# Left output products moved into the values pass and to the segment's end, and left products that lead only with resident units

## Chip, cores, metric

One core of one Trainium2 chip. The metric is the device time of one execution in us. The kernel before: 2348.51 us median of 3 runs (2346.82 to 2349.23). Every run lists the mean granted TensorE clock of the core. The views name the engines PE (TensorE), ACT (ScalarE), DVE (VectorE), POOL (GpSimd) and SP (SyncE, which issues the weight stream).

## The reference, cut to what matters

```python
for s in range(n_seg):                       # 64 segments of 32 tokens, one after the other
    xs = x[:, s * 32:(s + 1) * 32, :]
    h = concatenate([mem, xs])               # 8 memory rows + 32 token rows
    q, k, v = h @ Wq, h @ Wk, h @ Wv         # 1024 -> 32 heads x 128
    scores = where(mask, q k^T * scale, -1e9)
    o = softmax(scores) @ v
    o = o @ Wo                               # 4096 -> 1024
    mem = o[:, :8]                           # feeds the next segment
    outs.append(o[:, 8:])
# + x + gelu(xn @ w1 + b1) @ w2 + b2, xn = layernorm(x)
```

The layer norm and the dense part run first, in about 16% of the time. Then come the 64 segments. `mem` makes them a chain.

## The kernel before: what the argument touches

The weights are 64 units of 512 KB: eight units in each of K, Q, V for the first half of the heads, the same for the second half, then 16 output units. 43 stay resident in SBUF. 21 are streamed again in every segment, through six buffers.

```python
IS_STREAMED = {...}   # K 0,3,6; Q 1,4,7; V 2,5 of each half; output units 0,3,6,9,12

def unit_done(unit):
    if IS_STREAMED[unit]:
        start_stream()          # the buffer is free: the unit six places on is fetched
        ...
        # one or two small output writes are issued on POOL
```

Per segment, 24 token rows and the memory go through as "main" products (32 columns of weights loaded, hT). The last eight token rows of four segments in a row are joined into one "left" product (hL): left products are made in one segment of four. A segment has a kind 0 to 3 by its place in the group. Left K is made in kind 0, left Q in kind 2, left V in kind 3 (first half) and 0 (second half), left output in kind 3.

```python
def half_pass(w, u, left, at, lead=0):       # K is called with lead=3
    ...                                      # product() is left out
    for n in range(-lead, KT):
        if left and n + lead < KT:
            product(n + lead, hL, psL)       # leads by three units, streamed or not
        if n >= 0:
            product(n, hT, ps)
            unit_done((w, n, u))
            for fn in at.get(n, ()):
                fn()                         # attention steps between the products
    return ps, psL
...
lag = 3 if left_o else 0                     # output pass, kind 3
for n in range(16 + lag):
    if n < 16:
        o_product(n, [st["oT", 0], st.get(("oT", 1))], psX)
    if n == 15 and not final:
        nc.scalar.copy(out=o_sb[:, :], in_=psX[:, 0:256])   # making the tiles o_sb, res, resL is left out
    if left_o and n >= lag:
        o_product(n - lag, oL, psXL)         # left product, three units behind
    if n >= lag:
        unit_done(ORDER[48 + n - lag])
    for fn in at.get(n, ()):
        fn()
    if n == 7:
        nc.gpsimd.dma_start(out=res[:, :], in_=hr_d[s + 1, :, 256:512])
        if left_o:
            nc.gpsimd.dma_start(out=resL[:, :], in_=hrL_d[g + 1, :, 256:512])
if not final:
    put_mem(o_sb, nxt["hT"], ...)            # two transposes, DVE copy into hT: the new memory
nc.vector.tensor_tensor(out=res[:, :], in0=psX[:, 0:256], in1=res[:, :], op=ALU.add)
...                                          # with left_o, the addition for resL follows
```

The softmax here doesn't subtract the row's maximum and nothing guards it: scores larger than these inputs give would overflow.

Of the kernel before, what the change touches and what calls it, by code (L numbers as in the profile page):

```python
# [10 lines left out]
BF16 = mybir.dt.bfloat16  # L11
F32 = mybir.dt.float32
ACT = mybir.ActivationFunctionType
ALU = mybir.AluOpType
PSUM = bass.MemoryType.PSUM

P = 128
# [9 lines left out]
KT = DM // P  # L27
# [21 lines left out]
def pass_order():  # L49
# [14 lines left out]
ORDER = pass_order()  # L64
IS_STREAMED = {
    unit: (n * STREAMED + NUNIT - 1) // NUNIT != ((n + 1) * STREAMED + NUNIT - 1) // NUNIT
    for n, unit in enumerate(ORDER)
}
# [5 lines left out]
def kernel(  # L74
# [16 lines left out]
    nc = tc.nc  # L91
# [42 lines left out]
    for m, n, base in ((mask_order[0:NX, 0:NX], NX, 0), (mask_order[0:SEG, NX:SEG], NL, NX)):  # L134
        nc.gpsimd.affine_select(
            out=m, in_=m, pattern=[[1, n]], compare_op=ALU.is_ge, fill=MASKED, base=base, channel_multiplier=-1,
# [3 lines left out]
        out=m, in_=m, pattern=[[-8, GRP]], compare_op=ALU.is_ge, fill=MASKED, base=0, channel_multiplier=1,  # L140
    )
    nc.gpsimd.affine_select(
        out=m, in_=m, pattern=[[8, GRP]], compare_op=ALU.is_ge, fill=MASKED, base=7, channel_multiplier=-1,
# [58 lines left out]
    sp = ctx.enter_context(tc.tile_pool(name="sp", bufs=1))  # L202

    def put_mem(o_sb, hT, psM):

        for c in range(2):
            nc.tensor.transpose(psM[:, c, :], o_sb[:, c * P:(c + 1) * P], ident[:, :])
        nc.vector.tensor_copy(
            out=hT[:, :, NX:SEG].rearrange("p (j c) t -> p j c t", c=2),
            in_=psM[:, 0:2, :].rearrange("p c (j t) -> p j c t", j=4)[:, :, :, NX:SEG],  # L210
        )
# [3 lines left out]
    with tc.tile_pool(name="ma", bufs=2) as ma, tc.tile_pool(name="mps", bufs=6, space=PSUM) as mps:  # L215
# [11 lines left out]
        o_sb = sp.tile([P, 512], BF16, name="d")  # L227
# [18 lines left out]
        for i in range(14):  # L246
            t = slab(f"w2_{i}")[:, :].rearrange("p (c d) -> p c d", d=DM)
# [93 lines left out]
        for tg in range(4):  # L341
# [13 lines left out]
            for fb in range(FC):  # L355
                ps = mps.tile([P, 512], F32, name="ps")
                for kt in range(KT):
                    nc.tensor.matmul(  # L358
                        ps[:, :].rearrange("p (s t) -> p s t", t=SEG),
                        lhsT=w1_sb[fb // 14 * 8 + kt][:, (fb % 14) * P:(fb % 14 + 1) * P],  # L360
                        rhs=xnT[kt // 4][:, :, kt % 4, :],
                        start=(kt == 0),
                        stop=(kt == KT - 1),
# [3 lines left out]
                    out=xb[:, :], in_=ps[:, :], func=ACT.Identity, bias=b1col[:, fb:fb + 1], scale=1.0  # L367
                )
                u = ma.tile([P, 512], BF16, name="g_u")
                nc.vector.tensor_tensor(out=u[:, :], in0=xb[:, :], in1=xb[:, :], op=ALU.mult)  # L370
                nc.vector.tensor_scalar(
                    out=u[:, :], in0=u[:, :], scalar1=0.044715, scalar2=1.0, op0=ALU.mult, op1=ALU.add
# [7 lines left out]
            if tg == 0:  # L380
                for nb in range(2):
                    cs = slice(nb * 512, nb * 512 + 512)
                    ps = mps.tile([P, 512], F32, name="ps")
# [3 lines left out]
            if not last:  # L387
# [9 lines left out]
                for t in range(4):  # L397
# [3 lines left out]
                    for nb in range(2):  # L401
                        cs = slice(nb * 512, (nb + 1) * 512)
                        ps = mps.tile([P, 512], F32, name="ps")
# [56 lines left out]
    with tc.tile_pool(name="late", bufs=1) as late, \  # L460
# [7 lines left out]
        def unit_tile(unit):  # L468
            if IS_STREAMED[unit]:
                return stream_tiles.popleft()[:, :]  # L470
            return res_tiles[unit]
# [8 lines left out]
        def unit_done(unit):  # L480

            if IS_STREAMED[unit]:
                start_stream()
                if late_units:
                    fetch_late(late_units.popleft())
                for _ in range(2 if len(small) > 8 else 1):
                    if small:
                        small.popleft()()
# [6 lines left out]
        def by_head(t):  # L495
            return t.rearrange("p c (j t) -> p (c j) t", j=4)

        hT, hL = nxt["hT"], nxt["hL"]
        qL = qlp.tile([P, 8, P], BF16, name="qL")
        kL, VL, oL = [None] * 2, [None] * 2, [None] * 2  # L500
        for s in range(NSEG):
# [17 lines left out]
            def half_pass(w, u, left, at, lead=0):  # L519


                ps = accp.tile([P, 512], F32, name="acc")
                psL = accp.tile([P, 512], F32, name="acc") if left else None
                tiles = {}

                def product(i, lhs, acc):
                    if i not in tiles:
                        tiles[i] = unit_tile((w, i, u))
                    for j in range(4):
                        nc.tensor.matmul(  # L530
                            acc[32 * j:32 * j + 32, :],
                            lhsT=lhs[:, i, :],
                            rhs=tiles[i][:, 512 * j:512 * j + 512],
                            start=(i == 0),
                            stop=(i == KT - 1),
                            tile_position=(0, 32 * j),
                        )

                for n in range(-lead, KT):
                    if left and n + lead < KT:  # L540
                        product(n + lead, hL, psL)
                    if n >= 0:
                        product(n, hT, ps)
                        unit_done((w, n, u))
                        for fn in at.get(n, ()):
                            fn()
                return ps, psL

            def rows_out(ps, tag):
# [30 lines left out]
            def q_left(u):  # L580

                if i4 == 3 and more:
                    q = qS[:, u, :, :]
                else:
                    q = by_head(qL[:, 4 * u:4 * u + 4, :])[:, :, NL * i4:NL * i4 + NL]
                nc.vector.tensor_copy(out=st["qT"][:, :, 32:40], in_=q)
# [51 lines left out]
            def values(u, r):  # L638
# [22 lines left out]
                cp(out=st["oT", u][:, 2 * r:2 * r + 2, :, :], in_=oV[:, :, :, 0:32])  # L661
                cp(out=oL[u][:, 2 * r:2 * r + 2, :, NL * i4:NL * i4 + NL], in_=oV[:, :, :, 32:40])


            psK, psKL = half_pass("K", 0, left_k, {}, lead=3)
            nat = rows_out(psK, "d")
# [34 lines left out]
            if first:  # L701
                at[3].append(lambda: st.update(natL=left_out(psQ1L, "VL1", late)))
                at[5] = [lambda: turn_qL(st["natL"], 1), lambda: q_left(1)]
            else:
                at[3].append(lambda: q_left(1))
            psV1, psV1L = half_pass("V", 1, left_v[1], at)
            st["V"] = left_out(psV1, "a")
            if left_v[1]:
# [8 lines left out]
                at[8] = [lambda: st.update(natL=left_out(psQ1L, "d"))]  # L717
                at[11] = [lambda: turn_qL(st["natL"], 1)]
            psX = accp.tile([P, 512], F32, name="acc")
            psXL = accp.tile([P, 512], F32, name="acc") if left_o else None  # L720
            tiles = {}

            def o_product(n, lhs, acc):
                w, i, u = ORDER[48 + n]
                if n not in tiles:
                    tiles[n] = unit_tile((w, i, u))
                for k in range(2):
                    for jq in range(4):
                        nc.tensor.matmul(  # L729
                            acc[32 * jq:32 * jq + 32, 0:256],  # L730
                            lhsT=lhs[i // 4][:, i % 4, 2 * u + k, :],
                            rhs=tiles[n][:, 1024 * k + 256 * jq:1024 * k + 256 * jq + 256],
                            start=(n == 0 and k == 0),
                            stop=(n == 15 and k == 1),
                            tile_position=(0, 32 * jq),
                        )

            lag = 3 if left_o else 0
            res = resL = None
            for n in range(16 + lag):  # L740
                if n < 16:
                    o_product(n, [st["oT", 0], st.get(("oT", 1))], psX)
                if n == 15 and not final:
                    o_sb = sp.tile([P, 256], BF16, name="o_sb", tag="d")
                    nc.scalar.copy(out=o_sb[:, :], in_=psX[:, 0:256])
                if left_o and n >= lag:
                    o_product(n - lag, oL, psXL)
                if n >= lag:
                    unit_done(ORDER[48 + n - lag])
                for fn in at.get(n, ()):  # L750
                    fn()
                if n == 7:
                    res = sp.tile([P, 256], BF16, name="res", tag="e")
                    nc.gpsimd.dma_start(out=res[:, :], in_=hr_d[s + 1, :, 256:512])
                    if left_o:
                        resL = late.tile([P, 256], BF16, name="resL", tag="VL1")
                        nc.gpsimd.dma_start(out=resL[:, :], in_=hrL_d[g + 1, :, 256:512])
            if not final:
                put_mem(o_sb, nxt["hT"], trp.tile([P, 4, P], BF16, name="tr"))
            nc.vector.tensor_tensor(out=res[:, :], in0=psX[:, 0:256], in1=res[:, :], op=ALU.add)  # L760

# [2 lines left out]
                small.append(lambda o=o, r=res[32 * jq:32 * jq + NX, :]: nc.gpsimd.dma_start(out=o, in_=r))  # L764
            if left_o:
                rows_o = out_flat[g * GRP * SEG:(g + 1) * GRP * SEG, :].rearrange("(i t) d -> i t d", t=SEG)
                nc.vector.tensor_tensor(out=resL[:, :], in0=psXL[:, 0:256], in1=resL[:, :], op=ALU.add)

                for jq in range(4):
                    for i in range(GRP):  # L770
                        o = rows_o[i, NX:SEG, 256 * jq:256 * jq + 256]
                        r = resL[32 * jq + NL * i:32 * jq + NL * i + NL, :]
                        small.append(lambda o=o, r=r: nc.gpsimd.dma_start(out=o, in_=r))  # L773
# [37 lines left out]
```

## Time and profile before

| | before |
|---|---|
| time, median us | 2348.51 |
| TensorE busy, us | 2042.0 |
| moved by DMA, MB | 792.03 |
| group of four segments, mean us | 117.7 |
| kind 0, 1, 2, 3, mean us | 29.2, 28.1, 28.6, 31.8 |

The views are in the prediction. To read them: the stream of weights runs at about 407 GB/s when it is full (404 to 408 in the rows shown there). In one stretch of every group TensorE is nearly always busy and the stream starves (158 to 348 GB/s in the rows shown). That stretch goes from the output pass of kind 3 to V of the next kind 0.

### The profile page before, as it was taken

How to read it: one execution, taken by the hardware profiler on the slowest of the kernel's cores; microseconds unless marked ns; L12 is line 12 of the kernel's file. 1: busy time of each engine (PE TensorE's matmuls, PEld its weight loads, DVE VectorE, ACT ScalarE, POOL GpSimd, SP SyncE). 2: the span in 40 equal slices, each digit the busy share in tenths (PEclk: the TensorE clock that was granted, in tenths of full speed). 3: DMA queues.
4: the chain of work that ended last, by engine and by line, in shares of the span. 5: the costliest groups of instructions: out<-in, count | busy, mean ns of one | idle time of the engine just before them, and what ended most of it. 6: DMA issues, size and time to landing. Idle time of an engine off the chain costs nothing.

```text
span 2349.5 us, 84568 instructions
## 1 busy us (share of the span) xinstructions
PE 2042.0 (87%) x37759; PEld 1052.3 (45%) x37779; DVE 698.3 (30%) x1922; ACT 516.9 (22%) x1221; POOL 372.7 (16%) x745
## 2 busy tenths in 40 slices
PE   7999999788888888888888888888888888888885
PEld 3444444344444444444444444444444444444443
DVE  6574752122222222222222222222222222222221
ACT  5261432121111111111111211111111111111121
POOL 0000000023121212121212121212121212121212
PEclk9999999999999999999999999999999999999998
DMA  9521126899999999999999999999999999999996
GB/s 325 186 68 48 39 69 248 320 402 367 403 368 402 381 391 366 401 372 375 378 405 375 400 369 398 372 378 372 406 369 394 372 400 376 401 377 405 371 398 237
DMA packets 266408, 792.03 MB, mean 337 GB/s; under 512 B 55995, under 2 KB 71131, under 8 KB 266044
## 3 DMA queue, kind: packets, MB, share of 16 engines
q1 hardware_dynamic: 243004, 769.66, 85.2%
q0 software_dynamic: 22464, 15.92, 2.3%
q8 instruction: 295, 4.83, 0.8%
q10 hardware_dynamic: 576, 1.05, 0.1%
q14 instruction: 69, 0.57, 0.1%
HBM read 772.83 MB, written 29.88 MB: 342 GB/s over the span
## 4 chain that ended last, share of the span: by engine, by line
PE 49%; DMA 42%; issue 4%; DVE 3%; ACT 1%; POOL 1%; POOLq 0%; ACTq 0%; DVEq 0%; SPq 0%
DMA u<-Wc_Q 21%; PE acc L530 17%; DMA u<-Wc_O 11%; PE acc L729 9%; PE ps L358 8%; PE ps L405 6%; DMA u<-Wc_V 4%; DMA u<-Wc_K 3%; PE av L646 2%; DMA res<-hr_d 2%; PE tr L493 2%; PE ps L438 2%; PE av L652 1%; DVE natL L556 1%; PE pT L438 1%
## 5 line engine op out<-in xcount | busy, mean ns | idle before, releaser
L530 PE MATMUL acc<-u,hr 128*32 128x512 bf16 x12288 | 961.3, 388 | 111.0 <-DMA u<-Wc_Q 50.3
L530 PEld LDWEIGHTS <-hr 128*32 128x32 bf16 x12288 | 316.2, 96 | 434.5 <-issue 206.8
L530 PE MATMUL acc<-u,hrL 128*32 128x512 bf16 x3072 | 298.2, 384 | 22.2 <-DMA u<-Wc_V 10.3
L551 ACT CAST nat<-acc 128x512 bf16<-128x512 f32 x256 | 149.8, 585 | 558.9 <-PE acc L530 522.9
L729 PEld LDWEIGHTS <-oT 128*32 128x32 bf16 x8192 | 209.7, 97 | 93.1 <-issue 70.4
L729 PE MATMUL acc<-W_O,oT 128*32 128x256 bf16 x4096 | 184.2, 279 | 28.1 <-issue 27.9
L556 DVE CAST natL<-acc 128x512 bf16<-128x512 f32 x224 | 152.3, 686 | 187.1 <-PE acc L530 187.1
L729 PE MATMUL acc<-u,oT 128*32 128x256 bf16 x4096 | 186.1, 276 | 20.4 <-DMA u<-Wc_O 11.4
L358 PE MATMUL ps<-u 128*128 128x512 bf16 x896 | 196.2, 382 | 2.6 <-ACT u L282 2.6
L194 POOL DMA_DIRECT2D hr<-hr_d x63 | 35.0, 555 | 1010.9 <-PE acc L530 442.0
L764 POOL DMA_DIRECT2D out_dram<-res x256 | 129.3, 512 | 363.0 <-DVE res L760 359.6
L563 DVE COPY kT<-tr 128x512 bf16<-128x512 bf16 x128 | 54.3, 424 | 328.4 <-PE tr L493 328.4
L405 PE MATMUL ps<-u 128*128 128x512 bf16 x657 | 146.2, 379 | 0.8
L530 PEld LDWEIGHTS <-hrL 128*32 128x32 bf16 x3072 | 89.6, 96 | 106.9 <-issue 41.3
L358 PEld LDWEIGHTS <-u 128*128 128x128 bf16 x896 | 88.2, 98 | 109.3 <-issue 4.9
L773 POOL DMA_DIRECT2D out_dram<-resL x256 | 127.9, 505 | 51.8 <-DMA out_dram<-resL 26.2
L620 ACT ACTIVATE pr<-sm 128x224 bf16<-128x224 f32 x128 | 45.7, 357 | 387.5 <-PE sm L615 309.7
L575 DVE COPY qT<-tr 128x512 bf16<-128x512 bf16 x128 | 54.3, 424 | 250.0 <-PE tr L493 250.0
L661 DVE CAST oT<-av 128x256 bf16<-128x256 f32 x128 | 54.3, 424 | 211.7 <-PE av L652 211.7
L646 PEld LDWEIGHTS <-natL 32*128 32x128 bf16 x2048 | 76.8, 91 | 90.0 <-issue 53.9
L646 PE MATMUL av<-pr,natL 32*128 32x40 bf16 x2048 | 94.0, 177 | 15.2 <-DVE pr L634 9.9
L493 PEld LDWEIGHTS <-nat 128*128 128x128 bf16 x1024 | 58.1, 98 | 108.9 <-ACT nat L551 55.6
(100 smaller groups left out, 1825.3 us busy)
## 6 DMA issues: line engine op xcount, KB each, us to landing
u<-Wc_K SPq DMA_DIRECT2D x384, 512.0 KB, 7.0
u<-Wc_Q SPq DMA_DIRECT2D x384, 512.0 KB, 7.2
u<-Wc_O SPq DMA_DIRECT2D x320, 512.0 KB, 7.2
u<-Wc_V SPq DMA_DIRECT2D x256, 512.0 KB, 6.4
u<-in_B_w_dram SPq DMA_DIRECT2D x16, 448.0 KB, 5.5
u<-in_B_w_dram SPq DMA_DIRECT2D x14, 512.0 KB, 10.7
u<-in_A_Wv_dram SPq DMA_DIRECT2D x12, 512.0 KB, 7.9
u<-in_A_Wk_dram SPq DMA_DIRECT2D x10, 512.0 KB
```

The lines of the kernel that those rows point to most:

```text
L358: nc.tensor.matmul(ps[:, :].rearrange("p (s t) -> p s t", t=SEG), lhsT=w1_sb[fb // 14 * 8 + kt][:, (fb % 14) * P:(fb % 14 + 1) * P], rhs=x ...
L405: nc.tensor.matmul(ps[:, :], lhsT=gts[fc // 4][:, fc % 4, t * P:(t + 1) * P], rhs=w2_sb[fc // 2][:, fc % 2, cs], start=(fc == 0), stop=(fc ...
L438: nc.tensor.matmul(pss[2 * t + nb][:, :], lhsT=gts[fc // 4][:, fc % 4, t * P:(t + 1) * P], rhs=w2_sb[fc // 2][:, fc % 2, nb * 512:nb * 512 ...
L493: nc.tensor.transpose(dst[:, c, :], nat[:, c * P:(c + 1) * P], ident[:, :])
L530: nc.tensor.matmul(acc[32 * j:32 * j + 32, :], lhsT=lhs[:, i, :], rhs=tiles[i][:, 512 * j:512 * j + 512], start=(i == 0), stop=(i == KT - ...
L551: nc.scalar.copy(out=nat[:, :], in_=ps[:, :])
L556: nc.vector.tensor_copy(out=nat[:, :], in_=psL[:, :])
L563: nc.vector.tensor_copy(out=st["kT"][:, :, :], in_=by_head(tr[:, :, :]))
L646: nc.tensor.matmul(oV[:, b, c, :], lhsT=V[q, c * P:(c + 1) * P], rhs=prA[q, c, :], start=(c == 0), stop=False, skip_group_check=True, tile ...
L729: nc.tensor.matmul(acc[32 * jq:32 * jq + 32, 0:256], lhsT=lhs[i // 4][:, i % 4, 2 * u + k, :], rhs=tiles[n][:, 1024 * k + 256 * jq:1024 * ...
L764: small.append(lambda o=o, r=res[32 * jq:32 * jq + NX, :]: nc.gpsimd.dma_start(out=o, in_=r))
L773: small.append(lambda o=o, r=r: nc.gpsimd.dma_start(out=o, in_=r))
```

## The change

Its intent is that the streamed units of the output pass give their buffers back at once, and that left products fill TensorE where it waits. The left output products of the five resident units among the first eight go into the second values pass, those of the last three units (resident) after the last main product, and the other eight stay in the loop, without a lag. In K the left products that lead are of resident units, so the lead waits for no transfer. The order in the other half passes changes too: main first, then left.

```diff
+        O_UNITS = ORDER[48:]
+        O_LEFT = [unit for unit in O_UNITS[:8] if not IS_STREAMED[unit]], [], O_UNITS[-3:]
+        O_LEFT[1].extend(unit for unit in O_UNITS if unit not in O_LEFT[0] + O_LEFT[2])
...
+                ahead = [i for i in range(KT) if not IS_STREAMED[w, i, u]][:lead] if left else []
+                order = ahead + [i for i in range(KT) if i not in ahead]
...
-                for n in range(-lead, KT):
-                    if left and n + lead < KT:
-                        product(n + lead, hL, psL)
-                    if n >= 0:
-                        product(n, hT, ps)
-                        unit_done((w, n, u))
+                for i in ahead:
+                    product(i, unit_tile((w, i, u)), hL, psL, order)
+                for i in range(KT):
+                    t = unit_tile((w, i, u))
+                    product(i, t, hT, ps, range(KT))
+                    if left and i not in ahead:
+                        product(i, t, hL, psL, order)
+                    unit_done((w, i, u))
...
+            if left_o:
+                psXL = accp.tile([P, 512], F32, name="acc")
+                def o_lefts(k):
+                    for unit in O_LEFT[k]:
+                        o_product(unit, unit_tile(unit), oL, psXL, O_LEFT_SEQ)
+                at.setdefault(1, []).append(lambda: o_lefts(0))
             psV1, psV1L = half_pass("V", 1, left_v[1], at)
...
+            for n, unit in enumerate(O_UNITS):
+                t = unit_tile(unit)
+                o_product(unit, t, [st["oT", 0], st.get(("oT", 1))], psX, O_UNITS)
+                if left_o and unit in O_LEFT[1]:
+                    o_product(unit, t, oL, psXL, O_LEFT_SEQ)
+                unit_done(unit)
...
             if not final:
+                o_sb = sp.tile([P, 256], BF16, name="o_sb", tag="d")
+                nc.scalar.copy(out=o_sb[:, :], in_=psX[:, 0:256])
+            if left_o:
+                o_lefts(2)
+                nc.vector.tensor_tensor(out=resL[:, :], in0=psXL[:, 0:256], in1=resL[:, :], op=ALU.add)
+            if not final:
                 put_mem(o_sb, nxt["hT"], trp.tile([P, 4, P], BF16, name="tr"))
```

More of the change, by code (lines that the diff above doesn't have):

```diff
@@ L496, in by_head @@
             return t.rearrange("p c (j t) -> p (c j) t", j=4)
+        O_UNITS = ORDER[48:]
+        O_LEFT = [unit for unit in O_UNITS[:8] if not IS_STREAMED[unit]], [], O_UNITS[-3:]
+        assert not any(IS_STREAMED[unit] for unit in O_LEFT[2])
+        O_LEFT[1].extend(unit for unit in O_UNITS if unit not in O_LEFT[0] + O_LEFT[2])
+        O_LEFT_SEQ = [unit for units in O_LEFT for unit in units]
         hT, hL = nxt["hT"], nxt["hL"]
@@ L523, in half_pass, with product @@
                 psL = accp.tile([P, 512], F32, name="acc") if left else None
-                tiles = {}
-                def product(i, lhs, acc):
-                    if i not in tiles:
-                        tiles[i] = unit_tile((w, i, u))
+                ahead = [i for i in range(KT) if not IS_STREAMED[w, i, u]][:lead] if left else []
+                order = ahead + [i for i in range(KT) if i not in ahead]
+                def product(i, t, lhs, acc, seq):
                     for j in range(4):
@@ L532, in product @@
                             lhsT=lhs[:, i, :],
-                            rhs=tiles[i][:, 512 * j:512 * j + 512],
-                            start=(i == 0),
-                            stop=(i == KT - 1),
+                            rhs=t[:, 512 * j:512 * j + 512],
+                            start=(i == seq[0]),
+                            stop=(i == seq[-1]),
                             tile_position=(0, 32 * j),
                         )
-                for n in range(-lead, KT):
-                    if left and n + lead < KT:
-                        product(n + lead, hL, psL)
-                    if n >= 0:
-                        product(n, hT, ps)
-                        unit_done((w, n, u))
-                        for fn in at.get(n, ()):
-                            fn()
+                for i in ahead:
[6 more added lines that the diff above has]
+                    unit_done((w, i, u))
+                    for fn in at.get(i, ()):
+                        fn()
                 return ps, psL
@@ L662, in values, with o_product @@
                 cp(out=oL[u][:, 2 * r:2 * r + 2, :, NL * i4:NL * i4 + NL], in_=oV[:, :, :, 32:40])
+            def o_product(unit, t, lhs, acc, seq):
+                w, i, u = unit
+                for k in range(2):
+                    for jq in range(4):
+                        nc.tensor.matmul(
+                            acc[32 * jq:32 * jq + 32, 0:256],
+                            lhsT=lhs[i // 4][:, i % 4, 2 * u + k, :],
+                            rhs=t[:, 1024 * k + 256 * jq:1024 * k + 256 * jq + 256],
+                            start=(unit == seq[0] and k == 0),
+                            stop=(unit == seq[-1] and k == 1),
+                            tile_position=(0, 32 * jq),
+                        )
             psK, psKL = half_pass("K", 0, left_k, {}, lead=3)
@@ L719 @@
             psX = accp.tile([P, 512], F32, name="acc")
-            psXL = accp.tile([P, 512], F32, name="acc") if left_o else None
-            tiles = {}
-            def o_product(n, lhs, acc):
-                w, i, u = ORDER[48 + n]
-                if n not in tiles:
-                    tiles[n] = unit_tile((w, i, u))
-                for k in range(2):
-                    for jq in range(4):
-                        nc.tensor.matmul(
-                            acc[32 * jq:32 * jq + 32, 0:256],
-                            lhsT=lhs[i // 4][:, i % 4, 2 * u + k, :],
-                            rhs=tiles[n][:, 1024 * k + 256 * jq:1024 * k + 256 * jq + 256],
-                            start=(n == 0 and k == 0),
-                            stop=(n == 15 and k == 1),
-                            tile_position=(0, 32 * jq),
-                        )
-            lag = 3 if left_o else 0
-            res = resL = None
-            for n in range(16 + lag):
-                if n < 16:
-                    o_product(n, [st["oT", 0], st.get(("oT", 1))], psX)
-                if n == 15 and not final:
-                    o_sb = sp.tile([P, 256], BF16, name="o_sb", tag="d")
-                    nc.scalar.copy(out=o_sb[:, :], in_=psX[:, 0:256])
-                if left_o and n >= lag:
-                    o_product(n - lag, oL, psXL)
-                if n >= lag:
-                    unit_done(ORDER[48 + n - lag])
+            resL = None
+            for n, unit in enumerate(O_UNITS):
[4 more added lines that the diff above has]
+                unit_done(unit)
                 for fn in at.get(n, ()):
@@ L766 @@
                 rows_o = out_flat[g * GRP * SEG:(g + 1) * GRP * SEG, :].rearrange("(i t) d -> i t d", t=SEG)
-                nc.vector.tensor_tensor(out=resL[:, :], in0=psXL[:, 0:256], in1=resL[:, :], op=ALU.add)
                 for jq in range(4):
```

## The prediction

> **What bounds the kernel now.** I began with the page, because it says which resource is full.
>
> ```profile
> PE   7999999788888888888888888888888888888885
> DMA  9521126899999999999999999999999999999996
> GB/s 325 186 68 48 39 69 248 320 402 367 403 368 402 381 391 366 401 372 375 378 405 375 400 369 398 372 378 372 406 369 394 372 400 376 401 377 405 371 398 237
> ...
> q8 instruction: 295, 4.83, 0.8%
> ...
> PE 49%; DMA 42%; issue 4%; DVE 3%; ACT 1%; POOL 1%; POOLq 0%; ACTq 0%; DVEq 0%; SPq 0%
> ```
>
> From 16% of the span on, the 64 recurrent segments run. TensorE and the DMA engines are both nearly full, and the chain that ended last changes between the two. Each segment streams 21 weight units of 512 KB through six buffers. The rate swings between about 405 and 370 GB/s: segments differ. Four make a group, and "left" products (those that don't feed the memory) come in K of segment 0, Q of segment 2, values of segment 3 (first half) and 0 (second half), and the output of segment 3. From the copy that completes the memory (DVE, hr<-tr) to the next one, the four kinds take on average 29.2, 28.1, 28.6 and 31.8 us (trace, segments 4 to 59), 117.7 us a group.
>
> So I cut one segment 3 and the start of the next segment 0 into passes (second Q, second values, output, tail to the new memory; then K, Q, V, and the second K). The columns are length, busy time of PE, PEld, DVE, ACT and POOL, clock, DMA share and GB/s.
>
> ```profile
> 1490.94:1495.71 4.77, 3.27 (x72) 1.50 (x68) 0.47 (x2) 1.07 (x3) 0.00 (x0) 1.00 1.03 404
> 1495.71:1498.98 3.27, 3.16 (x75) 1.27 (x67) 1.63 (x5) 0.64 (x2) 0.00 (x0) 1.00 1.03 407
> 1498.98:1509.06 10.08, 8.15 (x271) 6.59 (x271) 1.70 (x5) 1.36 (x5) 1.62 (x3) 1.00 0.90 336
> 1509.06:1510.38 1.32, 1.32 (x44) 0.90 (x37) 0.19 (x2) 0.37 (x1) 0.00 (x0) 1.00 0.79 158
> 1510.38:1513.98 3.60, 3.46 (x64) 2.41 (x60) 0.68 (x3) 0.00 (x0) 2.96 (x6) 1.00 0.92 281
> 1513.98:1516.87 2.89, 2.75 (x45) 1.34 (x37) 1.02 (x2) 0.58 (x1) 2.05 (x5) 1.00 0.94 309
> 1516.87:1520.72 3.85, 3.29 (x77) 1.41 (x79) 1.39 (x4) 0.94 (x2) 2.52 (x5) 1.00 0.90 348
> 1520.72:1524.29 3.57, 3.57 (x66) 1.65 (x62) 0.74 (x3) 0.58 (x2) 2.50 (x5) 1.00 1.03 408
> ```
>
> The stream runs at 404 to 408 GB/s except from the output pass of segment 3 to V of segment 0, where TensorE is nearly always busy and the stream starves. Against 407 the five slow rows lose 1.76, 0.81, 1.11, 0.70 and 0.56 us, 4.9 us in this group. The chain shows the same stretch from inside:
>
> ```profile
> 1493.19 7.02 DMA u<-Wc_O
> ...
> 1503.27 1.74 PE acc L729 x57
> 1505.02 1.69 issue
> 1506.70 3.24 PE acc L729 x111
> 1509.94 0.22 PE tr L207 x2
> 1510.15 0.97 PE acc L530 x15
> ...
> 1511.27 2.78 PE acc L530 x46
> 1514.05 6.42 DMA u<-Wc_K
> ```
>
> It leaves a streamed output unit at 1500.2, goes through TensorE alone to 1514.05, and returns to a DMA issued when a K unit's buffer came free. In all 14 groups looked at, it leaves a Wc_O transfer some 10 to 12 us before the new memory. It re-enters the DMA by a transfer issued after it: a V unit twice (1.0 and 2.3 us), a K unit five times (3.2 to 4.7), a Q unit seven times (5.5 to 7.5). The change is worth only what it takes out of this stretch, or what it does to the first buffer releases after it.
>
> [...] in K, Q and V above, POOL issues small output writes for 2.0 to 3.0 us and the rate is 281 to 348, so not all of the loss there is the stream's own. [...] The blocks are here (q8: 295 of 16384 bytes), but not hidden: of 37 PE gaps over 0.5 us put down to "issue", most follow a block's landing by about 1.4 us, and fall 128 weight-load and matmul pairs apart. A block whose 128 pairs took 3.0 to 3.5 us is followed by a 1.7 us gap on average, one that took over 5 us by less than 0.2. [...]
>
> **The change part by part.** A unit is one 512 KB weight slab; its eight output matmuls start 0.22 us before the next unit's (1507.05, 1507.27, 1507.48 in the timeline), and so do the four matmuls of a K unit (1511.39, 1511.61).
>
> Work: no matmul is added or removed; both builds have 75560 PE rows. Five of the 16 left output products (resident units of the first eight) move into the second values pass, 5 x 0.22 = 1.1 us; eight stay in the loop; three come after it. Before, they lagged by three, so four came after the last main product: one fewer now.
>
> Inside the PE-bound stretch this moves time and saves none: the values pass above is 3.16 us busy of 3.27, so 1.1 us put there starts the output pass 1.1 us later. What it can absorb are DMA waits in values and output, on average 0.06 + 0.13 us a group: gain at most **0.2 us**.
>
> Releases in the output pass: streamed units are 0, 3, 6, 9, 12. Counted from the start of the values pass, with 0.22 us a product, the first is released 0.4 us later (1.1 us of moved work against a lag of three), the second at the same time, the last three 0.44, 0.66 and 0.66 us earlier. But these refill Q buffers, and Q never waits there; the stretch then ends in releases of K and Q units.
>
> Releases in K of segment 0: K0 comes after five products both ways; K3 after 9 instead of 11 (0.44 us earlier), K6 after 14 instead of 15 (0.22). A streamed unit lands not less than about 5.1 us after issue, and then 1.3 to 1.4 us apart, so the busy run of the DMA starts with the V units that K0 and K3 refill. V5's landing averages 8.0 us after the memory, PE wants it at about 8.2. I give **0.3 us**, an estimate, because half of the chains re-enter through Q units, whose releases don't move.
>
> Instruction blocks: boundaries stay at the same pair. I laid out the pairs of both orders at the start distances of the trace and summed 5.4 us less each block's length over all positions of the boundary: 4.5 us before, 4.4 after. Gain **0.1 us**.
>
> Costs: between sums and values in the output pass stand four products instead of five, and two or three instead of four around the two values steps; the waits for DVE pr that other segments show are 0.3 us. Loss **0.2 us**. At the end, the resL addition (0.41 us on DVE) now precedes the memory copy: left products 0.66, addition, copy 0.19, so about 1.5 to 1.6 us from the last main product to the first K product, where the three leading left products keep TensorE busy until 1.5: loss **0.1 us**. resL landed 0.7 us before the last main product on average (15 groups), latest 1.35 after it; the loop now ends 0.44 us sooner after its issue, so it is late in about one group of ten.
>
> Sum: 0.2 + 0.3 + 0.1 - 0.3 = 0.3 us a group, 16 groups: 5 us. As the releases in the output pass are also early for a stream that is starving, and I may have undervalued that, I put the centre at 0.55 us a group, 9 us: **2340 us**.
>
> **Rivals.** (1) The starving is cured: if earlier releases and an undelayed lead give back half of the 4.9 us, 16 x 2.4 = 39 us, 2309 us; all of it would be 2270. For it speaks the rate of 158 to 336 in just these windows; against it, that the PE work in the stretch is unchanged, so the transfers land earlier and are used no earlier. (2) The DVE order hurts: if resL is late by 1 us in half of the groups, and the shorter output loop waits for pr and oT, about 0.8 us a group, 2361 us. For it: DVE waited for res 45 times, 92 us in all; against it, resL's margin in segment 3. (3) Instruction blocks decide: one gap more or fewer a group, 1.7 us, is 27 us either way (2321 or 2376), since dense 256-column products are what makes them; the even spread of the boundaries over the groups speaks against it.
>
> **Range and chances.** The sum is small and its terms have errors of 0.2 to 0.5 us a group each, about 0.8 together, 13 us; the first rival in part stretches the lower side: 2320 to 2352. Over 2% faster needs 47 us, ten times my sum and most of the starved time: 0.04. Over 2% slower needs 3 us a group from waits of tenths: 0.02. Same: 0.94.
>
> **What would show it.** Right: the output pass of segment 3 some 1.1 us shorter, the values pass 1.1 us longer, their sum equal within 0.3; DMA rate in the tail and K still well under 400; issue gaps about 2 us a group in values and output together; V and K waits of segment 0 shorter by tenths; DVE's hr copy not waiting for resL. Wrong: a rate near 400 in the output pass and K with segments 3 and 0 over 1 us shorter together (first rival), main K products waiting for hr after resL (second), or issue gaps that double or vanish (third).

Numbers from the trace of the kernel before, for statements that stand there without one:

- In the K, Q and V rows of kind 0 the DMA engines were busy for a share of 0.90 to 0.94 and moved 281 to 348 GB/s; in the values row ahead of the output pass it was 1.03 and 407. That is what "not all of the loss there is the stream's own" goes by.
- "The blocks" are the 295 packets of 16384 bytes on queue q8, kind "instruction". TensorE has 75538 records, 256 to a block. After each of the 37 gaps it starts 1.2 to 1.6 us after a block's landing.
- Of the 37 gaps 29 stand ahead of output products (256 columns, L729), four ahead of L530 and four ahead of L652. That dense products make the gaps is the author's reading of this and of the lengths of the blocks.
- The 5.4 us is the estimate. Where a gap of over 0.5 us follows a block, block and gap together took 4.2 to 6.3 us, median 5.3.
- In Q of kind 0 TensorE has no wait of over 0.15 us for a Wc_Q transfer in 14 groups.
- The 5.1 us to landing is a misreading: it is the mean of one unit, the third Q unit, whose least is 4.2 (see the steps below).

## The result, and the profile after

2343.45 us median of 4 runs (2341.91 to 2347.8), against 2348.87 (2346.82 to 2350.11) for the kernel before. The ratio is 0.9981, 95% interval 0.9963 to 0.9998. Ratios are the mean time of one kernel's fast runs over that of the other's of the same rounds, so not quite the ratio of the medians quoted. In a second session the changed kernel gave 0.9969 (0.9948 to 0.9990).

**Part of the difference between the profiles is not the change.** The spans of the two profiled runs are 2349.5 and 2342.5 us, and 3.1 of these 7.0 us arose in code that the change doesn't touch. From the first memory copy to the first left product of the recurrence TensorE finishes the dense part: 54.6 us before, 51.4 after. Columns as in the prediction. The kernel before, first 13.6 us of it:

```profile
372.78:379.60 6.82, 6.82 (x16) 1.97 (x16) 0.00 (x0) 0.00 (x0) 0.00 (x0) 0.50 0.94 348
379.60:386.40 6.80, 6.75 (x32) 3.07 (x32) 0.00 (x0) 0.00 (x0) 0.00 (x0) 1.00 1.02 416
```

The changed kernel, the first 27.75 us:

```profile
372.25:400.00 27.75, 27.75 (x128) 12.32 (x128) 0.00 (x1) 0.00 (x0) 0.00 (x0) 1.00 1.00 396
```

For 6.8 us the granted clock was 0.50 and TensorE made 16 matmuls instead of 32. The dense part is the same in all kernels told of below; of their 12 profiled runs one, before_shift_64, has this window too. Such windows, most of them of 3.41 us, occur in both traces (17 before, 16 after, from 380 us on; the only shares of the clock in them are 0.5 and 1.0).

**The passes around the output.** A segment of kind 3 and the next of kind 0 of the changed kernel, cut at the same passes as in the prediction, from the second values pass to V:

```profile
1487.73:1491.95 4.22, 3.96 (x116) 2.39 (x111) 1.63 (x5) 0.59 (x1) 0.00 (x0) 1.00 1.03 409
1491.95:1500.01 8.06, 7.01 (x238) 5.84 (x234) 1.70 (x5) 1.42 (x5) 1.62 (x3) 1.00 1.00 378
1500.01:1504.12 4.11, 2.02 (x38) 0.80 (x30) 0.53 (x3) 0.37 (x1) 0.00 (x0) 1.00 0.87 304
1504.12:1508.67 4.55, 4.50 (x52) 1.92 (x56) 0.33 (x1) 0.00 (x0) 3.93 (x8) 0.62 0.61 186
1508.67:1511.48 2.81, 2.67 (x44) 1.11 (x36) 1.02 (x2) 0.58 (x1) 2.09 (x6) 1.00 1.02 322
1511.48:1514.18 2.70, 2.70 (x73) 1.31 (x75) 0.98 (x3) 0.58 (x1) 2.70 (x6) 1.00 0.92 326
```

The values pass is longer and the output pass shorter, as meant. But the tail (third row), 1.32 us before, took 4.11 here, with TensorE busy for 2.02. This is the worst of the groups. Over 14 groups (segments 4 to 59), in us:

| | values, second half | output | tail | K | Q | V | sum |
|---|---|---|---|---|---|---|---|
| before | 3.30 | 10.46 | 1.32 | 3.23 | 2.90 | 3.62 | 24.83 |
| after | 4.28 | 9.50 | 2.17 | 3.12 | 2.82 | 2.89 | 24.78 |

The chain of the changed kernel shows what the tail waits for:

```profile
1493.81 3.53 DMA u<-Wc_K
...
1497.39 0.42 POOL res L762
...
1497.93 5.57 DMA resL<-hrL_d
...
1503.59 0.06 DVE resL L771
...
1503.93 0.20 DVE hr L208
...
1504.17 5.54 PE acc L536 x68
```

And the timelines of DVE show the two orders (in brackets: how long the engine had been idle, and what ended that). Before:

```profile
1510.19 0.19 DVE L208 COPY hr<-tr 128x64 bf16<-128x64 bf16 x1 [6.32 <-PE tr L207]
1510.30 0.43 DVE L760 TENSOR_TENSOR res<-acc,res 128x256 bf16<-128x256 f32 x1
1510.64 0.41 DVE L767 TENSOR_TENSOR resL<-acc,resL 128x256 bf16<-128x256 f32 x1
```

After:

```profile
1503.59 0.42 DVE L771 TENSOR_TENSOR resL<-acc,resL 128x256 bf16<-128x256 f32 x1 [6.15 <-DMA resL<-hrL_d]
1503.93 0.18 DVE L208 COPY hr<-tr 128x64 bf16<-128x64 bf16 x1
1504.03 0.42 DVE L774 TENSOR_TENSOR res<-acc,res 128x256 bf16<-128x256 f32 x1
```

The memory copy, which every main product of the next segment needs, stands behind an addition that needs a DMA: DVE was idle for 6.15 us until the rows landed; the copy began 0.34 us after the addition had begun. In 15 groups the copy ended 2.06 us after the ACT copy of the main output began, where it ended after 1.28 us before. In the wait view of the changed kernel DVE waits for the rows of resL ten times (total, times, longest):

```profile
DVE resL L771 <- DMA resL<-hrL_d: 59.2, 10, 7.0
```

The total counts DVE's idle time from its last work on, so it isn't time on the path.

So the change fell into a loss that the prediction took for rare, and was still a little faster. That left two questions for experiments: what the wait costs, and which part of the change pays for it.

### The profile page after: what moved, and what is told of

Same layout as the page of the kernel before. It is cut to its first block, busy times and chain, and to the rows that moved or that the text cites. A ratio compares the mean times of both kernels' runs of the same rounds, so it can differ in the third digit from the quotient of the medians.

```text
span 2342.5 us, 84620 instructions
## 1 busy us (share of the span) xinstructions
PE 2037.6 (87%) x37779; PEld 1052.9 (45%) x37779; DVE 698.9 (30%) x1922; ACT 516.9 (22%) x1221; POOL 372.7 (16%) x745
## 4 chain that ended last, share of the span: by engine, by line
PE 50%; DMA 40%; issue 4%; DVE 3%; ACT 2%; POOL 1%; DVEq 0%; ACTq 0%; POOLq 0%; SPq 0%
DMA u<-Wc_Q 24%; PE acc L536 18%; PE ps L358 8%; PE acc L676 8%; PE ps L405 6%; DMA u<-Wc_O 5%; DMA u<-Wc_V 4%; DMA u<-Wc_K 3%; PE av L654 2%; DMA resL<-hrL_d 2%; PE tr L493 2%; PE ps L438 2%; PE av L660 1%; DVE natL L564 1%; DVE pr L642 1%
## 5 line engine op out<-in xcount | busy, mean ns | idle before, releaser
L676 PE MATMUL acc<-W_O,oT 128*32 128x256 bf16 x4096 | 177.6, 283 | 30.4 <-issue 30.2
L536 PEld LDWEIGHTS <-hrL 128*32 128x32 bf16 x3072 | 84.2, 97 | 65.4 <-issue 11.3
L493 PEld LDWEIGHTS <-nat 128*128 128x128 bf16 x1024 | 57.9, 98 | 103.8 <-issue 60.1
```

The source lines that it names most:

```text
L493: nc.tensor.transpose(dst[:, c, :], nat[:, c * P:(c + 1) * P], ident[:, :])
L536: nc.tensor.matmul(acc[32 * j:32 * j + 32, :], lhsT=lhs[:, i, :], rhs=t[:, 512 * j:512 * j + 512], start=(i == seq[0]), stop=(i == seq[-1] ...
L676: nc.tensor.matmul(acc[32 * jq:32 * jq + 32, 0:256], lhsT=lhs[i // 4][:, i % 4, 2 * u + k, :], rhs=t[:, 1024 * k + 256 * jq:1024 * k + 256 ...
```

## The experiments

All were correct, and were timed in 5 rounds against the kernel before on the same chip. Three sessions, on three chips; the kernel before had medians of 2351.32, 2348.07 and 2355.31 us in them, so only ratios compare. Their intervals are 0.0017 to 0.0028 either way, 4 to 7 us.

For the traces I use one more number, counted from the packet records of the weight queue (128 packets of 4096 bytes are a unit): the time from one unit's landing to the next. In a full stream it is 1.30 us. Eight units a group, from K0 of kind 0 to V5 of the same segment, take longer: 15.38 us before (standard error over 14 groups 0.17). I call them the starved eight. The other 76 units of the group took 102.45 us before (0.34), and 102.0 to 102.9 in all traces: no kernel differs clearly there. The packets of neighbouring units interleave, and how they are put to units moves these figures by up to 0.3 us: by order of time alone the starved eight are 15.31 us before, 15.16 and 14.83 in the two traces of the changed kernel and 14.08 in resL_early.

### after_again

The changed kernel once more, no edit.

> The changed kernel once more, as the yardstick for the other runs of this call. 2343.5 us, 2341 to 2348, as on record.

Measured 2343.86 us median, ratio 0.9969 (0.9948 to 0.9990). Starved eight 15.05 us (first trace 15.49): two traces of one kernel differ by as much as the kernels do. The gain of this program as it is built is small, but outside the noise in both sessions.

### resL_early

```diff
+                rowsL = sp.tile([P, 512], BF16, name="rowsL", tag="kL0")[:, 0:256]
+                nc.gpsimd.dma_start(out=rowsL, in_=hrL_d[g + 1, :, 256:512])   # before the second values pass
...
-                        nc.gpsimd.dma_start(out=resL[:, :], in_=hrL_d[g + 1, :, 256:512])
...
-                nc.vector.tensor_tensor(out=resL[:, :], in0=psXL[:, 0:256], in1=resL[:, :], op=ALU.add)
+                nc.vector.tensor_tensor(out=resL[:, :], in0=psXL[:, 0:256], in1=rowsL, op=ALU.add)
```

> The changed kernel, but the residual rows of the left outputs are loaded before the second values pass into a tile that is free there; the addition is where it was. In the changed kernel the addition waits for these rows in most of the 15 groups, and the copy of the memory, behind it on DVE, ends 2.06 us after the last main output product on average instead of the 1.18 us that it takes when the rows are there. Theory (that wait lies on the path): the copy ends at 1.2 us in every group, 0.9 us x 15 = 13 us less, 2330 us (2326 to 2334). Rival (the streamed units set the pace after the memory anyway, the wait is hidden behind them): the copy is as early, but K, Q and V of the next segment wait for transfers by as much longer; 2341 to 2345 us.

Measured 2345.51 us median, ratio 0.9976 (0.9948 to 1.0004). The wait is gone: the copy ends at 1.21 us, the tail is 1.26 us, and the starved eight are 14.31 us (0.16), the fewest of all traces. But the time isn't lower than that of after_again. My theory of 13 us fell. Not all of the rival shows either: V and K waits of the next segment did not grow by as much (V 3.06 us against 2.89 and 3.14). In this trace the other 76 units took 102.75 us. About 0.2 us of that is the load itself, moved to where the stream is full: the last streamed Q unit of kind 3 and the V unit behind it land 1.47 and 1.36 us after the unit ahead of them, before the edit 1.32 and 1.30 (the next expectation names another unit and 1.52). The rest is within the errors.

### resL_in_O

The same load, moved to the start of the output pass:

```diff
             if not final:
                 load_x_rows(s + 1, nc.gpsimd)
+            if left_o:
+                rowsL = sp.tile([P, 512], BF16, name="rowsL", tag="kL0")[:, 0:256]
+                nc.gpsimd.dma_start(out=rowsL, in_=hrL_d[g + 1, :, 256:512])
```

> As resL_early, but the rows are loaded at the start of the output pass, where the stream begins to starve, so that the load takes nothing from a full stream (in resL_early it did: the transfer of q4 of segment 3 took 1.52 us instead of 1.33). The tail is 1.3 us instead of 1.9 to 2.2, and the eight starved transfers of a group take 14.3 us as there instead of 15.3. Theory (the wait is on the path): 0.9 us x 15 = 13 us under the changed kernel: ratio to the kernel before 0.991 to 0.993. Rival (it is given back elsewhere, as the time of resL_early says): 0.996 to 0.999 with the rest of the group longer by what the starved stretch loses.

Measured 2341.84 us median, ratio 0.9966 (0.9942 to 0.9990): the rival's range. Copy at 1.29 us, tail 1.34 us, starved eight 14.89 us (0.23) where I expected 14.3. A part of what the tail gave came back in K: TensorE was idle for 0.25 us a group there, put down to "issue" (nothing that the profile shows was waited for), where the changed kernel had 0.00 to 0.06. From values to V the two kernels without the wait take 24.0 and 24.2 us a group, the two traces of the changed kernel 24.8 and 24.6; all four segments take 117.15 and 117.11 us against 117.46 and 117.31, with standard errors of 0.4 to 0.5. So the wait was on the chain, but 13 us of it did not reach the time. I can name only a small part: later instruction gaps. The remainder is below what these runs resolve.

### lead_only

The kernel before, with the half passes of the changed kernel.

```diff
-                for n in range(-lead, KT):
-                    if left and n + lead < KT:
-                        product(n + lead, hL, psL)
-                    ...
+                for i in ahead:
+                    product(i, unit_tile((w, i, u)), hL, psL, order)
+                for i in range(KT):
+                    ...                      # main, then left, as in the change
```

> The kernel before with the new half passes alone (left products lead only with resident units, left after main in the same unit); output pass as before. Theory: in K of segment 0 the third and sixth unit release their buffers 0.44 and 0.22 us earlier, V waits of segment 0 shrink from 0.43 us to 0.1 a group, and the first segment, in which weights still arrive, gains the 3.1 us that the two profiles show there: 0.3 x 15 + 3 = 7 us, 2342 us. Rival (the gain of the change is all from the output pass): 2348 us, first segment 104.6 us as before.

Measured 2343.62 us median, ratio 0.9972 (0.9947 to 0.9996): the theory's 2342, by time. The reason given was partly wrong. The 3.1 us of the first segment were the clock window shown above, not the half passes: the other traces have 101.2 to 101.6 us there, with old half passes too, except before_shift_64 (104.95), whose profile has the same window at 373.4 us. What remains is V of kind 0, whose waits for Wc_V fell from 0.29 to 0.14 us. But the issue gaps of kind 3 also fell, from 2.20 to 1.88 us a group, as those of the padded kernels do (below), so this run can't tell the order of products from the places of instructions.

### old_lead

The changed kernel, with the old lead (units 0, 1, 2, the first of them streamed).

```diff
-                ahead = [i for i in range(KT) if not IS_STREAMED[w, i, u]][:lead] if left else []
+                ahead = list(range(lead)) if left else []
```

> The changed kernel with the old lead in K: the first three units lead, the streamed one among them; the output pass is the new one. Theory: it loses what lead_only gains, at least the 3 us of the first segment: 2346 to 2350 us. Rival (the lead does nothing): 2343 us.

Measured 2344.65 us median, ratio 0.9970 (0.9947 to 0.9992): the rival. That the leading units are resident is worth nothing that can be seen. If the half passes matter, it is by the order, main before left, which this kernel keeps.

### output_only

The new output pass with the half passes of the kernel before, the reverse of lead_only.

```diff
-                for i in ahead: ...          # the change's half pass
+                for n in range(-lead, KT): ...   # as before
```

> The new output pass with the half passes of the kernel before (the other half of lead_only). If the two halves add up, and lead_only has the whole gain (ratio 0.9972 against 0.9969 for the changed kernel), this one is at the kernel before: ratio 0.999 to 1.002, time per group from landing to landing 117.6 to 117.9 us. Rival: either half gives the whole gain, as old_lead (0.997, new output pass with another lead) suggests: 0.996 to 0.998.

Measured 2348.77 us median, ratio 0.9996 (0.9971 to 1.0021). Taken by itself the new output pass gives nothing; it carries the resL wait (tail 1.82 us) and saves as much. At this point the gain seemed to be that of the half passes, but the next runs spoil that reading.

### before_shift_32 and shift_32

Instructions arrive in blocks: 295 packets of 16384 bytes on queue q8 in the kernel before, one for 256 of TensorE's 75538 records, or 128 pairs of weight load and matmul. From the segments' start on it has 37 issue gaps of over 0.5 us, 51.8 us in all. From one to the next they lie whole multiples of 128 pairs apart, to within three, and the first stands 94 pairs past a multiple of 128 in the traces of both kernels. So I take the boundaries to stay at fixed places in the program; then a pad ahead of the segments shifts them all.

```diff
         qL = qlp.tile([P, 8, P], BF16, name="qL")
+        for _ in range(32):
+            nc.tensor.transpose(qL[:, 0, :], ident[:, :], ident[:, :])
```

> The kernel before with the same 32 transposes; it is also a second profile of the kernel before's order. Theory: within 4 us of the kernel before (ratio 0.999 to 1.003), starved transfers 15.2 to 15.6 us a group, and the stretch between the first memory copy and the first K product of the recurrence at 51.4 us plus the transposes, because the 54.6 us in the first profile came of a granted clock of 0.87 there. Rival: 54.6 again (then something in the kernel before makes it), or over 8 us faster or slower (boundaries matter).

> The changed kernel with 32 unneeded transposes of the identity once ahead of the segments (their output is overwritten, results stay right), 2.6 us at most: every instruction block boundary in the segments falls 32 weight-load and matmul pairs earlier in the program. Theory (where the boundaries fall decides nothing, as both kernels already sample many positions): issue gaps in values and output of segment 3 stay at 2 us a group, ratio to the kernel before 0.996 to 0.999. Rival (the difference between the kernels is a matter of boundaries): gaps change by over 0.5 us a group and the time by over 8 us.

The 0.87 is the mean clock from 372.78 to 400 us of the first profile. Four transposes take 0.33 us in the trace of the kernel before (PE tr L493 x4), which makes about 2.6 us for 32 and 5.3 us for 64.

Measured, before with pad: 2341.85 us median, ratio 0.9974 (0.9949 to 0.9999). The theory (0.999 to 1.003) missed: the pad alone gave the kernel before as much as the change did. Changed kernel with pad: 2343.95 us, 0.9982 (0.9955 to 1.0009). The padded kernel before started its recurrence after 53.28 us, that is 51.4 and the transposes: that profile has no clock window there.

### before_shift_64, before_shift_16 and shift_16

The same edit, with 64 and 16 in place of 32.

> before_shift_32 was 0.9974 of the kernel before, as much as the whole change, though it only pads the program. With 64 transposes in place of 32 (5.2 us at most, ahead of the segments) the block boundaries of the segments fall half a block earlier; as a group is 17.5 blocks, that gives the even groups the places of the odd ones and leaves the set of places as in the kernel before. If the gain of before_shift_32 is of the places: back to the kernel before, ratio 0.999 to 1.002. If it is of the padding or of the start of the recurrence: 0.996 to 0.998. If it was noise: about 1.000 here too, and 1.000 for a pad of 16.

> A quarter of the way between the places of the kernel before and those of before_shift_32. If places decide: 0.997 to 1.000, issue gaps different from the 3.7 us a group of the kernel before. If before_shift_32 was noise: 0.999 to 1.001.

> The changed kernel with the same 16 transposes. With places 0 and 32 (shift_32) and before at 0, 32 and 16 this gives the change at three places: it was -5.5 and about +1 us, corrected for the clock. If the change is worth something of its own: 2 to 6 us under before_shift_16. If all of it is the places: equal to before_shift_16 within 2 us.

A group is 2240 pairs, 17.5 blocks, in the traces of both kernels.

Measured: before_shift_64 2354.48 us median, ratio 1.0003 (0.9985 to 1.0022); before_shift_16 2347.15 us, 0.9961 (0.9944 to 0.9978); shift_16 2348.77 us, 0.9968 (0.9947 to 0.9989). before_shift_64 is what places foresaw, before_shift_16 lies just below the range given for them (and 16 is half of the way to 32, not a quarter), and shift_16 equals before_shift_16 within the noise, the second of its cases.

The pad of 64, which by this count puts the boundaries back at the same set of places, gives the old time. Pads of 16 and 32 don't, and the intervals of 16 and 64 lie apart. That is what places would do; padding as such should have helped at 64 too. The table has the ratio to the unpadded kernel before:

| places | before | after | after over before |
|---|---|---|---|
| 0 | 1 (64: 1.0003) | 0.9969 | 0.9969 |
| 16 | 0.9961 | 0.9968 | 1.0007 |
| 32 | 0.9974 | 0.9982 | 1.0008 |
| mean | 0.9978 | 0.9973 | 0.9995 |

One caution: the profiles of places 0 and 64 both have the clock window in the dense part, 3.1 us, and those of 16 and 32 haven't. Whether the timed runs had it is not recorded, so a third to a half of the difference between places may be that window and not the blocks.

The last column's mean is 1 us in 2350, against errors of 2 to 3 us. The first session, not in the table, had 0.9981 for the change at place 0, which brings it nearer still to 1. The change gains at the one set of places where the kernel before is slow, and nothing that shows at the two others. I first looked at the sum of the issue gaps. A line of the wait view, TensorE only, from 476 to 2330 us, shows that it isn't the sum. The kernel before:

```profile
PE acc L729 <- issue: 44.5, 37, 2.6
```

before_shift_32:

```profile
PE acc L731 <- issue: 61.5, 53, 2.5
```

The faster one has more of them. Counted by kind of segment (gaps over 0.25 us, a group), kind 3 has 2.20 and 2.12 us with pads 0 and 64, and 1.93 and 1.80 us with pads 16 and 32; kinds 0 and 2 together have 0.81 and 1.35, then 1.59 and 1.94. The starved eight follow kind 3: 15.38 and 15.33 us, then 15.07 and 14.84. So the better pads move gaps from the stretch where TensorE sets the pace to segments where the stream does. Four kernels agree in this order; that it makes the 6 to 9 us is argued, not shown. In the changed kernel the same numbers (2.10 and 2.12, with pads 2.38 and 2.20) don't order the times.

### resL_in_O_at2

resL_in_O with one more edit: the early left products stand one unit later, so that they don't wait for the ACT copy of the queries.

```diff
-                at.setdefault(1, []).append(lambda: o_lefts(0))
+                at.setdefault(2, []).append(lambda: o_lefts(0))
```

In the changed kernel's timeline this wait stands in 15 of 16 groups; one ends with:

```profile
1488.59 0.84 PE L676 MATMUL acc<-u,oL 128*32 128x256 bf16 x24 [0.26 <-ACT nat L559]
```

> resL_in_O, and the early left products stand one unit later in the second values pass, so that they do not wait 0.26 us for the ACT copy of the queries as they do in every group of the changed kernel. That wait goes to 0; if the stretch from values to the next V is what the time follows, 0.26 x 15 = 4 us under resL_in_O, 0.994 to 0.996 of the kernel before; if, as with the wait for resL, little of it reaches the time, 0.996 to 0.997.

Measured 2340.21 us median (2336.85 to 2345.09), ratio 0.9934 (0.9918 to 0.9951), the fastest of all: 15 us under the kernel before of its session. The same place in its timeline has no wait ahead of it:

```profile
1490.04 0.84 PE L676 MATMUL acc<-u,oL 128*32 128x256 bf16 x24
```

and DVE's addition waits for TensorE alone, in all 16 groups:

```profile
DVE resL L773 <- PE acc L676: 81.3, 16, 7.3
```

The step from resL_in_O (0.9966) is 0.0032, 7 us, where 4 were expected (0.994 to 0.996); the two ran on different chips, and their intervals overlap. The trace doesn't show where the gain lies: values and output together take 13.46 us a group against 13.56 in resL_in_O, with standard errors of 0.2, and from values to V it is 24.3 us against 24.2. Its runs also had 0.0028 more granted clock than those of the kernel before in the same session, which goes with 3 us by the slope below. It was run at one set of places only, so some of its 15 us may be of the places too.

## Why the prediction was right

The time was foreseen as 2340 us with 2320 to 2352, and "same" as 0.94; it came out at 2343.45. By its own steps:

- **Work moves, none is saved.** Right, though the count of 75560 PE rows given for both builds is in no trace here (75538 rows before, 75558 after; some records are missing). Values and output together are 13.76 us before and 13.78 after; the parts moved by +0.98 and -0.96 us, foreseen 1.1. The moved units start 0.22 us apart as before.
- **The stream still starves after the change.** Right: 304 and 186 GB/s in tail and K above. The rival of cured starving (2270 to 2309 us) is refuted.
- **V and K waits of kind 0 shrink by tenths.** Right in size: V's waits for transfers fell from 0.43 to 0.06 us in the first trace, 0.20 in the second. The cause given, resident units in the lead, is not borne out: old_lead has 0.13 without it. A reading under this step was off: 5.1 us is not the least time in which a starved unit lands but the mean of one such unit, the third Q unit (4.2 at the least; seven landings are known). The page's medians over all units whose landing is known are 6.4 us (V) to 7.2 us (Q and output).
- **Instruction gaps about 2 us in values and output.** Right, 2.01 to 1.89 us. But the term was treated as if the boundaries sampled all places evenly. They don't: an even spread was the reason for setting the third rival aside, and before_shift_16 and before_shift_64 show a difference of 0.4% between places, part of which may be the clock window. The rival as put (1.7 us a group) is too large; at a third of that it was as large as my centre.
- **resL late in about one group of ten.** Wrong: this step failed. It was waited for in ten of 16 groups. I took its landing from the kernel before (0.74 us ahead of the ACT copy) and moved it by the 0.44 us that the loop shortens. It moved by 1.72 us, to 0.98 after. The issue came 0.66 us later relative to the end, and the load took 5.31 us instead of 4.25, in an output pass where the mean rate rose from 341 to 373 GB/s. A load's duration was carried over from a pass with a starved stream to one with a fuller stream.
- **The tail costs 0.1 us.** Wrong by the same cause: 0.8 us. That is the second rival's event, almost to its size (0.8 us a group), but not its consequence of 2361 us, because removing it changed the ratio by +0.0007 (resL_early against after_again) and -0.0003 (resL_in_O, another session), not by the 0.0055 that 13 us are.

So the total was right, and the traces bear out its main reason: the stretch is bound by TensorE, whose work stayed the same (24.83 us before, 24.78 after). No run takes TensorE work out of the stretch, so that its length sets the time is not tested by itself. Its small terms were not right. The sum of 0.3 to 0.55 us a group came near the 5.4 us measured with two terms missing that nearly cancel at this program's places: a tail 0.7 us worse than foreseen, whose price was mostly not paid, and a gain tied to the places.

What stays open: where the 13 us that the resL wait should have cost are made up. The clock is one candidate. Over the 109 timed runs, with a mean for each kernel and session, 0.01 of granted clock goes with 11.7 us. That is as large as all effects here and differs from run to run. Nor do the windows of half clock fall just anywhere. I cut the recurrence of both traces, from 480 to 2320 us, into windows of 3.41 us in step with them. All 11 windows in which TensorE, by its records, was idle for 2.0 us or more were followed by half clock, and 19 of the 1067 others. In the 3.41 us ahead of each stretch of half clock TensorE was idle for 1.0 to 2.5 us in all (at 564.0 us of the kernel before after one gap of 2.50, at 1424.1 after one of 1.49 and shorter ones). One such window took K in the group shown above (0.62), after 2.05 us of idle time in the tail. That the idle time makes the half clock is not shown, but it would give a wait of TensorE a second price.

## What to carry to other kernels

Here the stretch that sets the time was full of one engine's work, and moving that work within it and releasing buffers earlier changed it from 24.83 to 24.78 us a group: in such a case look for what shortens the stretch itself. (The fastest kernel here took out a wait of 0.26 us that repeats in every group, but its trace does not show that this made the gain.) Before an addition is put ahead of a copy on the path on the same engine, ask what the addition waits for: here the copy ended 2.06 us after the ACT copy began instead of 1.28. Take the duration of a load from a place where the queues are as full as they will be: the same 64 KB took 4.25 us before and 5.31 after. And before a gain of 0.3% is credited to an edit, pad the program without changing it: here 16 or 32 unneeded transposes gave as much (0.9961 and 0.9974, against 0.9969 for the change).
